# A decode layer streamed through two buffers: a branch to a stub at TensorE's start, one odd row loaded whole, and repeated products in two gaps

## The chip, the core and the metric

The kernel runs on one core of one Trainium2 chip. A core has TensorE (PE in the profile), VectorE (DVE), ScalarE (ACT), GpSimd (POOL) and SyncE (SP), which here issues nearly all the loads, and 16 DMA engines that carry them. The metric is the device time of one execution in microseconds; lower is better. A change of about 0.3% is what a measurement of this kernel can tell from none.

## The reference

One decode step of a transformer layer, in float32, for a batch of 8 tokens with 1024 features:

```python
xn = layernorm(x)                                  # x: 8 x 1024
q = xn @ wq                                        # 32 heads of 128
k, v = last 1024 positions of the caches           # 4 key/value heads, each for 8 heads
p = softmax(q @ k.T * 128 ** -0.5)
h = x + (p @ v) @ wo                               # wo: 4096 x 1024
hn = layernorm(h)
out = h + (gelu(hn @ w_gate) * (hn @ w_up)) @ w_down    # Df = 3584
```

The weights and the caches are 111 MB, each byte of which is used once; the activations are small.

## The kernel before

**Stages.** The weights are rearranged on the host into loads of 128 partitions x 64 KB (8 MB), and two SBUF buffers take them in turn. A pass of TensorE's loop (line 500) uses both: half a (buffer 0, accumulators ob[0]) and half b (buffer 1, ob[1]). The passes are wq, the keys, the values, wo, gate and up for 2048 columns (GU0), gate and up for the other 1536 (GU1, pass 5), and the down projection (DN, pass 6), which has a half a only. W_down has 28 blocks of 128 rows: the first 8 travel in the unused quarter of GU1's loads, 16 are DN's half a, and the last four come behind it.

**A half.** `products` (line 481) goes through 8 steps of four products. The four of a step stand side by side in the array, each with 32 columns of the stationary operand, and write four groups of 32 partitions of an accumulator. Before the steps listed in `cuts` TensorE waits. DN's loads come in three pieces, wd0, wd1 and wd2 (5, 2 and 1 steps; `CUTS`), and TensorE waits ahead of steps 0, 5 and 7. Between the halves `turn` (line 470) transposes the activations. What TensorE waits for is collected by GpSimd, which waits for the semaphores in TensorE's order and raises a single one, `go` (lines 452 to 462).

**Repeated products.** At the places in `AGAIN` TensorE repeats a product with the residual whose result is in fin already (line 479), n times in a small loop: two ahead of DN's step 0 and two ahead of its step 5, and four ahead of step 4 of GU1's half b. They change nothing in the output.

**The start.** The loop runs from -1: pass -1 skips the body (line 501) and goes from the loop's end back to its start.

**The loads.** SyncE issues all loads in a written order; one that needs a buffer waits for TensorE's mark that the buffer is free. Behind wd2 come, into buffer 1, the blocks of W_down's last four rows of blocks (from here on rows): the odd row, two single rows (512 KB each, ws1 and ws2), and the last row in two pieces (256 KB each, we0 and we1). The odd row's first half is one load of 128 partitions (w_odd, 256 KB). Its second half (w_low) is folded to 64 partitions of 4 KB and comes in eight loads of 8 partitions, 32 KB each (line 202), at partitions p0, p0 + 4, ... for the p0 of `OFFSETS`. A load of 128 partitions is spread over all 16 DMA engines, each of these over eight. Fifteen tiny loads (`tag`, line 218) follow, which no computation uses.

**The tail.** The odd row makes three products into ob[0] (line 536): one of 128 partitions in column group 0, and for the folded half two of 64 partitions in groups 2 and 3; ScalarE copies the activations of partitions 64 to 127 to at_low for the last one (line 415). VectorE adds ob[0] to d1 (line 427). Then TensorE sums into fin: row ws1, d1 through add2, row ws2 (line 528), and the last row's pieces (line 547). ScalarE copies fin out in two halves (line 431), which two DMAs store.

Of the kernel before, what the change touches and what calls it, by code (L numbers as in the profile page):

```python
# [30 lines left out]
EARLY = 8  # L31
ENDS = (128, 128)
SINGLE = 3
LOW = P // 2
OFFSETS = (0, 1, 2, 3, 32, 33, 34, 35)
TAGS = 15
AGAIN = (((0, DN, 2), (CUTS[1], DN, 2)), ((STEPS // 2, GU1, 4),))


class Flow:  # L40
# [57 lines left out]
    def run(self, engine, make, *waits, mark=True):  # L98
        ins = self.start(engine, make, waits)
        if not mark:  # L100
            return None
        self.done[engine] += 1
        ins.then_inc(self.own[engine], 1)
        self.tell(engine, self.own[engine], self.done[engine])
        return self.own[engine], self.done[engine]

    def move(self, name, out, src, *waits, engine="sync"):
        s = self.sem(name)
        self.start(engine, lambda e: e.dma_start(out, src), waits).then_inc(s, 16)
        self.tell(engine, s, 16)  # L110
        return s, 16
# [19 lines left out]
    return out  # L131


def decode_block(nc, x, w, dn, side, single, ends, outs):
    fl = Flow(nc)
    run, move = fl.run, fl.move
    scale = DH ** -0.5
# [45 lines left out]
    for k in range(1, DN):  # L183
# [11 lines left out]
    landed[DN, 0] = [  # L195
        move(f"wd{i}", buf[0][:, a * NQ * N:b * NQ * N], dn[i], pe(f"a{GU1}"))
        for i, (a, b) in enumerate(zip(CUTS, CUTS[1:]))]
    w_odd, w_low = buf[1][:, 0:N], buf[1][0:LOW, N:N + D]
    odd_in = [move("wo0", w_odd, single[0], pe(f"b{GU1}"))]
    low_in = fl.sem("w_low")  # L200
    for j, p0 in enumerate(OFFSETS):
        nc.sync.dma_start(w_low[p0:p0 + 29:4], side[j]).then_inc(low_in, 16)
    odd_in.append((low_in, 16 * len(OFFSETS)))
    singles = []
    for i in range(1, SINGLE):
        t = buf[1][:, N + i * D:N + (i + 1) * D]
        singles.append((t, move(f"ws{i}", t, single[i])))
    blocks = []
    c0 = 0
    for i, (n, src) in enumerate(zip(ENDS, ends)):  # L210
        a = N + SINGLE * D + NQ * c0
        t = buf[1][:, a:a + NQ * n]
        blocks.append((n, t, move(f"we{i}", t, src)))
        c0 += n
# [158 lines left out]
    at_low = sb("at_low", LOW, 32)  # L373
    wide = st[0].rearrange("p (i c m) -> p i c m", i=STEPS, c=2)

    def widen(i0, i1, *ready):
# [88 lines left out]
    def wait():  # L465
        nc.tensor.wait_ge(go, 1).then_inc(go, -1)  # L466
# [4 lines left out]
    def turn(src):  # L471
        for i in range(NC):
            ins = nc.tensor.transpose(t8[:, i, :], src[:, i * P:(i + 1) * P], ident)  # L473
        marked(ins)
# [22 lines left out]
            if i % (STEPS // 2) == STEPS // 2 - 1:  # L497
                marked(ins)

    with nc.Fori(-1, PASSES, engines=[mybir.EngineType.PE]) as it:  # L500
        with nc.tensor.If(it >= 0):
            wait()
            turn(xs[1])
            products(0, CUTS)
            with nc.tensor.If(it < DN):
                wait()
                turn(xs[0])
                products(1, (0, STEPS // 2))
                with nc.tensor.If(it == WO):
                    wait()  # L510
                    for ch in range(2):
                        ins = nc.tensor.matmul(
                            fin[0:ROWS, ch * N:(ch + 1) * N], to_rows[:, ch, :], y_sb,
                            start=True, stop=True)
                    marked(ins)
                    wait()
                    for ch in range(2):
                        ins = nc.tensor.matmul(  # L518
                            fin[64 * ch:64 * ch + 32, ch * N:(ch + 1) * N],
                            spread.rearrange("p r b -> p (r b)"), h_sb[:, ch * N:(ch + 1) * N],  # L520
                            start=True, stop=True)
                    marked(ins)

    def add(lhs, rhs, *waits, start=False):

        for d_ps, a, b in halves:
            for j in range(NQ):
                run("tensor", lambda e: e.matmul(  # L528
                    d_ps[32 * j:32 * j + 32, :], lhs(j), rhs(j)[:, a:b], start=start, stop=False),
                    *waits, mark=False)  # L530

    odd = LAST - SINGLE
    for i, (q, lhs, t) in enumerate((
            (0, at[:, odd, :], w_odd), (2, at[0:LOW, odd, :], w_low[:, 0:N]),
            (3, at_low, w_low[:, N:2 * N]))):
        tok = run("tensor", lambda e: e.matmul(  # L536
            ob[0][32 * q:32 * q + 32, N:2 * N], lhs, t, start=False, stop=True,
            skip_group_check=True), *odd_in, at_ok, low_ok, mark=(i == 2))
# [80 lines left out]
```

## Time and profile before

| | |
|---|---|
| timed runs | 267.45, 267.75, 268.28 us; median 267.75 |
| profiled execution | 265.81 us, span 264.5 us |
| granted TensorE clock, mean | 0.826 |
| PE busy | 147.1 us (56%) in 1030 instructions |
| DVE, ACT, POOL busy | 28.5, 28.7, 5.3 us |
| read from HBM | 111.19 MB, 421 GB/s over the span |
| queue q1 (SyncE's loads) | 97.9% of 16 engines |
| queue q8 (instruction) | 2 packets, 0.03 MB |

The profile is of one execution. Busy time is given by engine and by line; the timeline lists instructions in order of time, merged where neighbours are alike, with what an engine was idle for in brackets. PE is the matmul part of TensorE, PEq its instruction queue. The chain that ended last is followed back only to 249.32 us, to the start of the down projection. The granted clock says which share of TensorE's full speed the throttle allowed in a stretch. "Us to landing" is the time from a DMA's issue to its last byte.

### The profile page before, as it was taken

Reading aid. Unit: us, or ns where it says so; the run is one execution under the profiler, and the core shown is the slowest. Engines: PE = TensorE matmul, PEld = TensorE weight load, DVE = VectorE, ACT = ScalarE, POOL = GpSimd, SP = SyncE. Lnnn points to the kernel's source line nnn. Section 1 sums busy time; section 2 is a strip of 40 time slices with the busy share of each in tenths; the row PEclk is TensorE's granted clock in tenths of the full one; section 3 lists DMA queues with packets and bytes.
Section 4 is the critical chain, followed back from the end, with each engine's and each line's share of the span. In section 5 each row is a group of like instructions: output and inputs, shape, how many; then the busy total and the mean of one; then the engine's idle time right before and its main releaser. Section 6 shows DMA issues by size and latency. Waiting matters only on the chain. (4 is left out here: it accounts for less than half of the span.)

```text
span 264.5 us, 2418 instructions
## 1 busy us (share of the span) xinstructions
PE 147.1 (56%) x1030; PEld 50.4 (19%) x1030; DVE 28.5 (11%) x47; ACT 28.7 (11%) x50; POOL 5.3 (2%) x11
## 2 busy tenths in 40 slices
PE   0023924814915926617617808728909609957696
PEld 0021311211211221111112302103302202312222
DVE  0310020010010010400400100250000200102011
ACT  1030000020030030010010000033200100200200
POOL 8000000000000000000000000000000000000000
PEclk9999995985985865965975976985885968997999
DMA  8998999899799979998999899799979999999894
GB/s 320 471 456 347 466 476 426 377 466 476 337 466 466 476 327 466 476 456 347 466 476 426 377 466 476 337 466 466 476 322 466 406 456 416 421 429 477 378 402 144
DMA packets 3843, 111.37 MB, mean 421 GB/s; under 512 B 696, under 2 KB 952, under 8 KB 1664
## 3 DMA queue, kind: packets, MB, share of 16 engines
q1 hardware_dynamic: 3680, 111.23, 97.9%
q10 hardware_dynamic: 160, 0.10, 0.1%
q8 instruction: 2, 0.03, 0.1%
q14 instruction: 1, 0.01, 0.0%
HBM read 111.19 MB, written 0.13 MB: 421 GB/s over the span
## 5 line engine op out<-in xcount | busy, mean ns | idle before, releaser
L493 PE MATMUL o<-w,st 128*32 128x512 f32 x832 | 118.0, 725 | 76.5 <-PEq L466 70.1
L493 PEld LDWEIGHTS o<-w,st 128*32 128x32 f32 x832 | 33.0, 130 | 153.0 <-issue 152.9
L473 PE MATMUL tt<-ident,zeros 128*128 128x128 f32 x104 | 16.5, 311 | 36.0 <-PEq L466 36.0
L473 PEld LDWEIGHTS tt<-ident,zeros 128*128 128x128 f32 x104 | 13.3, 159 | 46.4 <-issue 46.4
L479 PE MATMUL fin<-zeros,spread 128*32 128x512 f32 x16 | 7.4, 594 | 0.0
L330 DVE SCALAR_TENSOR_TENSOR av<-o,rtot,own 128x512 f32<-128x512 f32 x4 | 3.0, 750 | 31.3 <-PE o L493 31.3
L313 DVE TENSOR_REDUCE nmax<-o 128x1 f32<-128x1024 f32 x2 | 2.4, 1224 | 35.3 <-PE o L493 35.3
L340 ACT COPY st<-tt 128x512 f32<-128x512 f32 x4 | 2.1, 588 | 35.4 <-PE tt L473 35.4
L315 ACT ACTIVATE zeros<-o,nmax 128x1024 f32<-128x1024 f32 x2 | 2.2, 1114 | 33.6 <-DVE nmax L313 33.6
L355 DVE TENSOR_TENSOR y_sb<-o,y_sb 128x512 f32<-128x512 f32 x3 | 2.1, 692 | 34.2 <-PE o L493 34.2
L295 DVE SCALAR_TENSOR_TENSOR zeros<-o,tq 128x512 f32<-128x512 f32 x2 | 1.4, 692 | 36.1 <-PE o L493 36.1
L399 DVE TENSOR_TENSOR u<-o,u 128x512 f32<-128x512 f32 x2 | 1.4, 692 | 31.8 <-PE o L493 31.8
L390 DVE TENSOR_TENSOR g<-o,g 128x512 f32<-128x512 f32 x2 | 1.4, 691 | 29.4 <-PE o L493 29.4
L294 ACT ACTIVATE tq<-o 128x512 f32<-128x512 f32 x2 | 1.2, 597 | 23.9 <-PE o L493 23.9
L333 DVE TENSOR_REDUCE zeros<-av 128x128 f32<-128x1024 f32 x2 | 3.7, 1872 | 0.1
L362 ACT COPY zeros<-fin 32x512 f32<-32x512 f32 x1 | 0.6, 574 | 26.4 <-PE fin L518 26.4
L226 POOL MEMSET zeros<- 128x3712 f32 x1 | 3.2, 3191 | 0.0
L405 ACT COPY at<-tt 128x512 f32<-128x512 f32 (+1 forms) x2 | 1.1, 532 | 19.3 <-PE tt L473 19.3
L389 ACT COPY g<-o 128x512 f32<-128x512 f32 x2 | 1.2, 586 | 16.2 <-PE o L493 16.2
L262 ACT ACT_TABLE_LOAD x2 | 2.6, 1283 | 2.9 <-POOL ident L223 2.9
L278 ACT COPY st<-tt 128x1024 f32<-128x1024 f32 x2 | 2.0, 1012 | 7.7 <-PE tt L473 7.7
L398 ACT COPY u<-o 128x512 f32<-128x512 f32 x2 | 1.2, 586 | 14.4 <-PE o L493 14.4
(60 smaller groups left out, 43.6 us busy)
## 6 DMA issues: line engine op xcount, KB each, us to landing
w<-ends SPq DMA_DIRECT2D x4, 4096.0 KB, 23.4
w<-ends SPq DMA_DIRECT2D x1, 5120.0 KB, 22.8
w<-ends SPq DMA_DIRECT2D x1, 2048.0 KB, 27.3
w<-ends SPq DMA_DIRECT2D x1, 1024.0 KB, 29.3
w<-ends SPq DMA_DIRECT2D x2, 512.0 KB, 10.6
w<-ends SPq DMA_DIRECT2D x3, 256.0 KB, 11.3
w<-ends SPq DMA_DIRECT2D x8, 32.0 KB
w<-w SPq DMA_DIRECT2D x10, 29.3
```

The lines of the kernel that those rows point to most:

```text
L226: clear = run("gpsimd", lambda e: e.memset(zeros, 0.0))
L262: tok = run("scalar", lambda e: e.activation(sd, ve, AF.Sqrt), tok)
L278: a = run("scalar", lambda e: e.copy(st[0].rearrange("p (c r b) -> p c r b", c=NC, b=B), xt.unsqueeze(2).to_broadcast([P, NC, P // B, B])) ...
L313: tok = run("vector", lambda e: e.tensor_reduce(out=nmax, in_=ob[s], axis=AX.X, op=ALU.max, negate=True), pe(f"{h}1"))
L315: tok = run("scalar", lambda e: e.activation(xs[s], ob[s], AF.Exp, bias=nmax, accum_out=tot), tok)
L330: tok = run("vector", lambda e: e.scalar_tensor_tensor(av[:, i], o3, rtot, own.unsqueeze(2).to_broadcast([P, HB, DH]), op0=ALU.mult, op1=A ...
L333: tok = run("vector", lambda e: e.tensor_reduce(out=out, in_=av.rearrange("p i b d -> p d (i b)"), axis=AX.X, op=ALU.add), tok)
L340: tok = run("scalar", lambda e: e.copy(heads[:, g], turned.unsqueeze(2).to_broadcast([P, REP, P // 2 // B, B])), pe(f"t{h}2"))
L355: tok = run("vector", lambda e: e.tensor_add(y_sb, part, y_sb), ready, tok)
L473: ins = nc.tensor.transpose(t8[:, i, :], src[:, i * P:(i + 1) * P], ident)
L479: nc.tensor.matmul(fin[0:32, 0:N], spread.rearrange("p r b -> p (r b)"), h_sb[:, 0:N], start=True, stop=True)
L493: ins = nc.tensor.matmul(ob[s][32 * r:32 * r + 32, c:c + N], st[s][:, i * P + 32 * r:i * P + 32 * r + 32], buf[s][:, (i * NQ + r) * N:(i * ...
```

## The change

Four things are done.

1. The loop runs from 0, without a test for pass -1. Ahead of it TensorE branches to a block "far", which holds only a branch to "near", where the loop begins. "far" is written inside the test for pass `WO`, behind its products; a branch to "behind" goes around it.
2. The odd row isn't folded. It is loaded as one load of 128 partitions x 4 KB, as the single rows are, so buffer 1 holds three single rows, and w_odd, w_low and the eight small loads go.
3. The odd row makes two products of 128 partitions, in column groups 0 and 2; at_low and its copy go.
4. `AGAIN`: DN has three repeated products ahead of step 0 and none ahead of step 5; GU1's half b has six.

The core of the diff:

```diff
-LOW = P // 2
-OFFSETS = (0, 1, 2, 3, 32, 33, 34, 35)
-AGAIN = (((0, DN, 2), (CUTS[1], DN, 2)), ((STEPS // 2, GU1, 4),))
+AGAIN = (((0, DN, 3),), ((STEPS // 2, GU1, 6),))
...
-    w_odd, w_low = buf[1][:, 0:N], buf[1][0:LOW, N:N + D]
-    odd_in = [move("wo0", w_odd, single[0], pe(f"b{GU1}"))]
-    low_in = fl.sem("w_low")
-    for j, p0 in enumerate(OFFSETS):
-        nc.sync.dma_start(w_low[p0:p0 + 29:4], side[j]).then_inc(low_in, 16)
-    odd_in.append((low_in, 16 * len(OFFSETS)))
     singles = []
-    for i in range(1, SINGLE):
-        t = buf[1][:, N + i * D:N + (i + 1) * D]
-        singles.append((t, move(f"ws{i}", t, single[i])))
+    for i in range(SINGLE):
+        t = buf[1][:, i * D:(i + 1) * D]
+        singles.append((t, move(f"ws{i}", t, single[i], pe(f"b{GU1}"))))
...
-            low_ok = run("scalar", lambda e: e.copy(at_low, at[LOW:P, LAST - SINGLE, :]), at_ok)
...
-    with nc.Fori(-1, PASSES, engines=[mybir.EngineType.PE]) as it:
-        with nc.tensor.If(it >= 0):
+    only = [mybir.EngineType.PE]
+    entry = nc.cur_bb
+    nc.tensor.br("far")
+    nc.switch_bb("near")
+    with nc.Fori(0, PASSES, engines=only) as it:
...
+                nc.tensor.br("behind")
+                with nc.body("far", parent=entry, valid_engines=only):
+                    nc.tensor.br("near")
+                nc.switch_bb("behind")
...
-    for i, (q, lhs, t) in enumerate((
-            (0, at[:, odd, :], w_odd), (2, at[0:LOW, odd, :], w_low[:, 0:N]),
-            (3, at_low, w_low[:, N:2 * N]))):
+    for ch in range(2):
         tok = run("tensor", lambda e: e.matmul(
-            ob[0][32 * q:32 * q + 32, N:2 * N], lhs, t, start=False, stop=True,
-            skip_group_check=True), *odd_in, at_ok, low_ok, mark=(i == 2))
+            ob[0][64 * ch:64 * ch + 32, N:2 * N], at[:, odd, :], t[:, ch * N:(ch + 1) * N],
+            start=False, stop=True, skip_group_check=True), here, at_ok, mark=(ch == 1))
```

The built programs are listed by engine, in the order in which the instructions stand. TensorE at the loop's start, before; COMPARE_AND_BRANCH of L501 is the test for pass -1, the rows of L487 to L478 are the repeated products ahead of steps 0 and 5:

```order
L500 UNCONDITIONAL_BRANCH
L501 COMPARE_AND_BRANCH
L473 MATMUL tt<-ident,zeros 128x128 x8
L487 COMPARE_AND_BRANCH
L478 UNCONDITIONAL_BRANCH
L479 MATMUL fin<-zeros,spread 32x512
L478 REGISTER_ALU
L478 COMPARE_AND_BRANCH
L487 UNCONDITIONAL_BRANCH
L493 MATMUL o<-w,st 32x512 x20
L487 COMPARE_AND_BRANCH
L478 UNCONDITIONAL_BRANCH
```

The same place after (L492 is the branch ahead of the loop, L494 the loop):

```order
L492 UNCONDITIONAL_BRANCH
L494 UNCONDITIONAL_BRANCH
L463 MATMUL tt<-ident,zeros 128x128 x8
L477 COMPARE_AND_BRANCH
L468 UNCONDITIONAL_BRANCH
L469 MATMUL fin<-zeros,spread 32x512
L468 REGISTER_ALU
L468 COMPARE_AND_BRANCH
L477 UNCONDITIONAL_BRANCH
L483 MATMUL o<-w,st 32x512 x32
```

The test for pass -1 is gone, and the products of steps 0 to 7 stand in one piece. TensorE at the loop's end and the start of the tail, before (L512 and L518 are pass `WO`'s products, L500 the loop's end, L536 the odd row, L528 the sums):

```order
L509 COMPARE_AND_BRANCH
L512 MATMUL fin<-y_sb,zeros 64x512 x2
L518 MATMUL fin<-zeros,spread 32x512 x2
L509 UNCONDITIONAL_BRANCH
L500 REGISTER_ALU
L500 COMPARE_AND_BRANCH
L536 MATMUL o<-w,at 32x512 x2
L536 MATMUL o<-w,at_low 32x512
L528 MATMUL fin<-w,at 32x128 x8
L528 MATMUL fin<-d,add 32x128 x8
```

And after:

```order
L502 COMPARE_AND_BRANCH
L505 MATMUL fin<-y_sb,zeros 64x512 x2
L511 MATMUL fin<-zeros,spread 32x512 x2
L516 UNCONDITIONAL_BRANCH
L494 REGISTER_ALU
L494 COMPARE_AND_BRANCH
L532 MATMUL o<-w,at 32x512 x2
L525 MATMUL fin<-w,at 32x128 x8
L525 MATMUL fin<-d,add 32x128 x8
```

The branch to "behind" (L516) stands where the test's own branch stood; a row of the stub's branch (line 518) is not among TensorE's. The odd row has two products instead of three. SyncE's loads from wd0 on, before:

```order
L109 DMA w0<-ends 128x10240
L109 DMA w0<-ends 128x4096
L109 DMA w0<-ends 128x2048
L109 DMA w1<-ends 128x512
L202 DMA w1<-ends 8x1024 x8
L109 DMA w1<-ends 128x1024 x2
L109 DMA w1<-ends 128x512 x2
```

And after:

```order
L107 DMA w0<-ends 128x10240
L107 DMA w0<-ends 128x4096
L107 DMA w0<-ends 128x2048
L107 DMA w1<-ends 128x1024 x3
L107 DMA w1<-ends 128x512 x2
```

Nine loads, of the odd row in two forms, have become one. The bytes are the same.

More of the change, by code (lines that the diff above doesn't have):

```diff
@@ L131, in pe_order, with decode_block @@
     return out
-def decode_block(nc, x, w, dn, side, single, ends, outs):
+def decode_block(nc, x, w, dn, single, ends, outs):
     fl = Flow(nc)
@@ L210, in decode_block @@
     for i, (n, src) in enumerate(zip(ENDS, ends)):
[L211 removed]
+        a = SINGLE * D + NQ * c0
         t = buf[1][:, a:a + NQ * n]
@@ L498, in products @@
                 marked(ins)
-    with nc.Fori(-1, PASSES, engines=[mybir.EngineType.PE]) as it:
-        with nc.tensor.If(it >= 0):
+    only = [mybir.EngineType.PE]
[3 more added lines that the diff above has]
+    with nc.Fori(0, PASSES, engines=only) as it:
+        wait()
+        turn(xs[1])
+        products(0, CUTS)
+        with nc.tensor.If(it < DN):
             wait()
-            turn(xs[1])
-            products(0, CUTS)
-            with nc.tensor.If(it < DN):
+            turn(xs[0])
+            products(1, (0, STEPS // 2))
+            with nc.tensor.If(it == WO):
                 wait()
[L507 to L522, printed above, removed]
+                for ch in range(2):
+                    ins = nc.tensor.matmul(
+                        fin[0:ROWS, ch * N:(ch + 1) * N], to_rows[:, ch, :], y_sb,
+                        start=True, stop=True)
+                marked(ins)
+                wait()
+                for ch in range(2):
+                    ins = nc.tensor.matmul(
+                        fin[64 * ch:64 * ch + 32, ch * N:(ch + 1) * N],
+                        spread.rearrange("p r b -> p (r b)"), h_sb[:, ch * N:(ch + 1) * N],
+                        start=True, stop=True)
+                marked(ins)
+                nc.tensor.br("behind")
+                with nc.body("far", parent=entry, valid_engines=only):
+                    nc.tensor.br("near")
+                nc.switch_bb("behind")
     def add(lhs, rhs, *waits, start=False):
@@ L530, in add @@
                     *waits, mark=False)
+    (t, here), *singles = singles
     odd = LAST - SINGLE
[L533 to L535 removed]
+    for ch in range(2):
         tok = run("tensor", lambda e: e.matmul(
[L537 to L538 removed]
+            ob[0][64 * ch:64 * ch + 32, N:2 * N], at[:, odd, :], t[:, ch * N:(ch + 1) * N],
+            start=False, stop=True, skip_group_check=True), here, at_ok, mark=(ch == 1))
     assert tok == odd_done
@@ L585 @@
     parts += [main[:, a * NQ:b * NQ] for a, b in zip(CUTS, CUTS[1:])]
-    odd = down[:, LAST - SINGLE]
-    low = odd[:, 1].reshape(2, LOW, N).transpose(1, 0, 2)
-    parts += [np.stack([low[p0:p0 + 29:4] for p0 in OFFSETS]), odd[:, 0]]
-    parts += [down[:, i] for i in range(LAST - SINGLE + 1, LAST)]
+    parts += [down[:, i] for i in range(LAST - SINGLE, LAST)]
     parts += [row[:, :, a:b] for a, b in zip(cuts, cuts[1:])]
@@ L609 @@
     w = [aps["w"][i] for i in range(2 * GU1)] + small[0:4]
-    dn, side, single, ends = small[4:7], small[7], small[8:8 + SINGLE], small[8 + SINGLE:]
-    side = side.rearrange("p n -> (p n)").rearrange("(j r n) -> j r n", j=len(OFFSETS), r=8)
-    decode_block(nc, aps["x"], w, dn, side, single, ends, outs)
+    dn, single, ends = small[4:7], small[7:7 + SINGLE], small[7 + SINGLE:]
+    decode_block(nc, aps["x"], w, dn, single, ends, outs)
     r = run_bass_kernel_spmd(nc, [arrays], core_ids=[0])
```

1 line of the change is left out of this document (removed).

## Prediction

> **What bounds the kernel now.** I read the page's slices and queues first, then TensorE's timeline from 226 us, the DMA issues, and the busy time in stretches of 3.41 us.
>
> The page: what the DMA engines do, and what each load takes from issue to landing.
>
> ```profile
> DMA  8998999899799979998999899799979999999894
> q1 hardware_dynamic: 3680, 111.23, 97.9%
> q8 instruction: 2, 0.03, 0.1%
> w<-ends SPq DMA_DIRECT2D x1, 5120.0 KB, 22.8
> w<-ends SPq DMA_DIRECT2D x1, 2048.0 KB, 27.3
> w<-ends SPq DMA_DIRECT2D x1, 1024.0 KB, 29.3
> w<-ends SPq DMA_DIRECT2D x2, 512.0 KB, 10.6
> w<-ends SPq DMA_DIRECT2D x3, 256.0 KB, 11.3
> ```
>
> The loads fill 16 engines almost all the time: up to the last 15 us the kernel is a stream of 111 MB that TensorE waits for. Only the tail, after the last large load, can be shortened by an engine. SyncE's timeline gives the issue times to add to these waits.
>
> ```profile
> 226.43 16.53 SPq L109 DMA_DIRECT2D w<-ends  x4
> 248.50 1.86 SPq L109 DMA_DIRECT2D w<-ends  x4
> ```
>
> The first three of the four at 226.43 are the W_down loads wd0, wd1 and wd2, about 0.44 us apart, so they land at 226.43 + 22.8 = 249.2, 226.87 + 27.3 = 254.2 and 227.31 + 29.3 = 256.6. The four at 248.50 stand 0.46 apart; the last lands at 249.90 + 11.3 = 261.2.
>
> TensorE's timeline from the up projection to the end (start, us, what):
>
> ```profile
> 230.95 3.60 PE L479 MATMUL fin<-zeros,spread 128*32 128x512 f32 x8
> 237.25 5.34 PE L493 MATMUL o<-w,st 128*32 128x512 f32 x32 [2.69 <-PEq L466]
> 244.32 1.06 PE L473 MATMUL tt<-ident,zeros 128*128 128x128 f32 x8 [1.74 <-PEq L466]
> 245.32 1.90 PE L479 MATMUL fin<-zeros,spread 128*32 128x512 f32 x4
> 249.36 4.50 PE L493 MATMUL o<-w,st 128*32 128x512 f32 x40 [2.14 <-PEq L466]
> 253.65 1.45 PE L479 MATMUL fin<-zeros,spread 128*32 128x512 f32 x3
> 254.94 0.59 PE L479 MATMUL fin<-zeros,spread 128*32 128x512 f32 x1
> 254.97 3.14 PE L493 MATMUL o<-w,st 128*32 128x512 f32 x21
> 257.94 1.56 PE L536 MATMUL o<-w,at 128*32 128x512 f32 x3
> 259.35 0.59 PE L536 MATMUL o<-w,at_low 64*32 64x512 f32 x1
> 260.81 0.65 PE L528 MATMUL fin<-d,add 128*32 128x128 f32 x16 [0.29 <-DVE mark L434]
> 261.70 0.62 PE L547 MATMUL fin<-w,at 128*32 128x128 f32 x16
> ```
>
> Four products stand side by side in the array and take two passes; I call one pass of four a slot. Ten slots (x40) run from 249.36 to 253.65, so a slot is 0.43 us at full clock. A repeated product is two slots that use a quarter of the array. From 249.36 the chain is: five steps (10 slots), two repeated products (4 slots), steps 5 and 6 (4), step 7 (2), the odd row (L536), an add on VectorE, and sums. Its end is set by TensorE: the last load is there at 261.2, TensorE reaches the last sums at 261.70. VectorE and ScalarE close it:
>
> ```profile
> 260.06 0.69 DVE L427 TENSOR_TENSOR d<-o,d 128x512 f32<-128x512 f32 x1 [6.24 <-PE o L536]
> 262.17 0.48 ACT L431 COPY o_fin<-fin 128x128 f32<-128x128 f32 x2 [14.74 <-PE fin L547]
> 262.69 0.35 ACTq L109 DMA_DIRECT2D out<-o_fin  x1
> ```
>
> The profiled execution took 265.81 us (span 264.5). The three timed runs took 267.45 to 268.28, median 267.75: 1.6 to 2.5 us more. I sum against 265.81 first and come back to that gap, because the change acts on it.
>
> **The branch and the stub.** The rows of TensorE's order hold the branch of line 492 and nothing of line 518: the stub is an empty detour that the program no longer contains, and TensorE goes straight into pass 0. [...]
>
> ```profile
> q8 instruction: 1, 0.02, 5.2%
> ```
>
> One 16 KB fetch takes 5.2% of 16 engines for 1.1 us, 0.92 us of one engine, in the stream. [...] What it is late by at the end can be read from the DMA share (columns: stretch, its length, busy us of PE, PEld, DVE, ACT and POOL with counts, granted PE clock, DMA share, GB/s):
>
> ```profile
> 257.20:258.20 1.00, 1.00 (x10) 0.22 (x2) 0.00 (x0) 0.00 (x0) 0.00 (x0) 1.00 1.04 410
> 259.40:260.20 0.80, 0.80 (x16) 0.33 (x16) 0.14 (x1) 0.00 (x0) 0.00 (x0) 1.00 0.59 225
> 260.60:261.20 0.60, 0.39 (x16) 0.40 (x20) 0.15 (x2) 0.00 (x0) 0.00 (x0) 1.00 0.07 8
> ```
>
> From 259.4 on 0.59 of 16, nine engines, still read. Eight are those of the small loads, which gave each 8 x 4 KB = 32 KB that the others don't have; the ninth has only been late all along, by about as much as 32 KB take. 111.23 MB in 97.9% of 264.5 us are 430 GB/s, 27 per engine, so 32 KB take 1.2 us. I take 1.2 us for the lag, before and after, since it is the whole effect of such a fetch in this stream; its lower bound is the packet alone, 0.92, its upper bound is rival 4.
>
> **No small loads.** On SyncE eight issues and w_odd's become one, which brings the later issues from 248.50 to about 243.5; their data come behind wd2, 256.6, either way, so the data stream hides it. What changes is the late engine's share: 512/16 = 32 KB for the odd row where it had 256/16 = 16 KB. That is +0.6 us on it from there on. The odd row lands at 256.6 + 1.2 = 257.8, the last block at 261.2 + 0.6 = 261.8.
>
> The odd row itself gets shorter. Today the 128-row product and the two 64-row products don't overlap: 257.94 to 259.35 + 0.59 = 259.94, 2.00 us. Two 128-row products in different columns share slots, as those of L493 do: 2 slots, 0.43 + 0.59 = 1.02 us. (If they did not overlap it would be 4 slots, 1.9 us: that is the upper bound, and no loss against today.) Also the ScalarE copy into at_low goes, 0.22 us that wait for nothing.
>
> Sum at this execution's clock: start 257.8 + 0.1 = 257.9, end 258.9, add on VectorE (0.12 later, 0.69 long) to 259.75, its sums from 259.8 instead of 260.81. Now the loads come last: the last block at 261.8, its eight instructions 0.1 later, their last start about 261.95 to 262.0 where today it is 262.05. So 1.0 us won on TensorE is given back to the late engine and the end moves by -0.1 us: 265.7.
>
> **The repeated products.** Three instead of two ahead of the down projection end 0.86 us later, at 248.1, still before 249.2: free here. Six instead of four in the up projection fill 230.95 to 236.1, the load is used from 237.25: free too. Two in the middle of the last pass go: 4 slots, 1.7 us, off the chain. At this execution's clock that shows as little (steps 5 to 7 then wait for wd1 at 254.2 and wd2 at 256.6, and end at 257.8 instead of 258.1). It shows when the clock is low. Granted clock and TensorE's busy time in stretches on which the clock changes (same columns):
>
> ```profile
> 70.58:73.99 3.41, 1.50 (x16) 0.27 (x8) 1.23 (x1) 0.58 (x1) 0.00 (x0) 1.00 0.84 365
> 73.99:77.40 3.41, 1.07 (x8) 0.86 (x8) 0.16 (x1) 1.63 (x3) 0.00 (x0) 1.00 0.75 327
> 77.40:80.81 3.41, 0.00 (x0) 0.00 (x0) 0.00 (x0) 0.00 (x0) 0.00 (x0) 0.50 1.38 596
> 179.80:183.22 3.42, 2.15 (x14) 0.57 (x16) 0.00 (x0) 2.06 (x2) 0.00 (x0) 0.50 0.75 326
> 183.22:186.63 3.41, 3.41 (x24) 0.91 (x20) 0.00 (x0) 0.00 (x0) 0.00 (x0) 0.50 1.15 500
> 217.35:220.76 3.41, 2.85 (x16) 0.90 (x20) 0.00 (x0) 0.00 (x0) 0.00 (x0) 0.50 1.03 442
> 220.76:224.18 3.42, 3.42 (x36) 1.07 (x32) 0.00 (x0) 0.59 (x1) 0.00 (x0) 1.00 0.96 412
> 234.41:237.83 3.42, 0.72 (x9) 0.34 (x12) 0.00 (x0) 0.00 (x0) 0.00 (x0) 1.00 0.88 381
> 237.83:241.24 3.41, 3.41 (x24) 1.09 (x16) 0.00 (x0) 0.00 (x0) 0.00 (x0) 0.50 1.20 517
> 241.24:244.66 3.42, 1.68 (x15) 0.53 (x8) 1.38 (x2) 0.00 (x0) 0.00 (x0) 1.00 1.03 443
> ```
>
> The changes fall on a grid of 3.41 us. Full clock falls to half behind a stretch with 0.72 or 1.07 us of work and holds behind 1.50; half clock holds behind 2.15 us of work and rises behind 2.85. I put the limits between: 1.3 us to fall, 2.5 us to rise. Nothing ties this grid to the kernel's start in the rows, so in another execution it may lie elsewhere. Put it 1.1 us later. Then 235.51 to 238.92 holds 1.7 us of work, the clock stays full, and the four steps from 237.25 take 3.6 instead of 5.34 us. Everything up to the repeated products is 1.75 us earlier; they end at 245.5. The stretch 245.76 to 249.17 is empty, and 249.17 to 252.58 runs at half clock: 3.22 us / 0.86 = 3.8 slots, the other 6.2 at 0.43, five steps done at 255.3 instead of 253.65. Ten more slots bring the odd row to 259.55 instead of 257.94. From there on all is one chain: the end is 1.6 us later. That is about the gap between 265.81 and the timed median. Working the same steps through for 18 places of the grid, the kernel before ends 1.4 to 2.5 us later in 12 of them.
>
> After the change the same place gives: six repeated products until 236.1, full clock, three until 246.3, half clock from 249.17 too, five steps done at 255.3. But then only six slots follow: step 7 leaves the array at 257.9, when the odd row's load lets it start anyway. The cost is nothing; over the 18 places it is at most 0.1 us.
>
> [...]
>
> **The rivals.** (1) Forecast: the timed runs before are mostly at such places of the grid. Then 267.75 - 1.6 - 0.1 = 266.05, say 266.1. For it: the gap has the right size in all three runs (1.64, 1.94, 2.47). Against it: one profiled execution shows one place only. Chance 0.52.
>
> (2) The gap is something else that profiled and timed executions differ by, and stays. Then only the -0.1 us counts: 267.65, no change that can be told (0.3%, 0.8 us, is about what a measurement of this kernel can tell). Chance 0.35.
>
> (3) The stub is run after all, and the fetch comes before the stream instead of inside it: in the trace it lies at 5 us, a few us behind the first load's start. The late engine then isn't late, every load lands up to 1.2 us earlier: 264.9 on top of (1), 266.45 on top of (2). Against it: the order has no such branch. Chance 0.03.
>
> [...] Chance 0.10. [...]
>
> **How the numbers follow.** The time is that of (1), 266.1. Its own range is 265.2 (a place that costs 2.5 today) to 266.4 (1.4, with a lag of the upper half). The range must reach (2), 267.65 with 0.25 around it: 265.2 to 267.9. Faster by over 0.3% takes (1) and (3), 0.55; the same is (2), 0.35; slower is (4), 0.10.
>
> **What would show it.** Right: a 16 KB fetch away from 5 us, near 45; odd products of about 1.0 us; the sums on d before 260.2; the last sums waiting for their load; a span of 264.2 to 264.6 wherever the clock's changes lie, with five steps at half clock costing nothing. Wrong: a fetch at 2 us or none, several fetches, a last landing after 262.2, or timed runs that again lie 2 us above the profiled one.

## The result, and the profile after

The changed kernel takes 265.71 us (median of five runs, 265.51 to 265.87) where the kernel before takes 267.45 in the five runs beside it (267.28 to 268.28): a ratio of 0.9928, 95% interval 0.9912 to 0.9944. The profiled execution took 265.51 us with a span of 264.0; before it was 265.81 and 264.5. So the two profiles lie 0.3 us apart, the timed runs 1.7. Where the other 1.4 us are, no comparison of the two profiles can show.

The page of the changed kernel: the DMA slices, the queues, the chain that ended last, and the loads (us from issue to landing).

```profile
DMA  8997998999799979999997999799989999999994
...
q8 instruction: 2, 0.03, 0.1%
...
DMA 7%; PE 2%; SPq 1%; issue 0%; ACT 0%
DMA w<-ends 7%; PE o L483 1%; SPq L107 1%; PE fin L543 0%; ACT o_fin L421 0%
...
w<-ends SPq DMA_DIRECT2D x3, 512.0 KB, 17.8
...
w<-ends SPq DMA_DIRECT2D x2, 256.0 KB, 18.9
```

SyncE's timeline (start, us, what):

```profile
227.01 15.99 SPq L107 DMA_DIRECT2D w<-ends  x8
```

The chain that ended last now consists mostly of loads (DMA 7% of the span, TensorE 2%); before, it was TensorE's work from the down projection on. The small loads take longer from issue to landing because they are issued earlier: all eight loads by 243.0, where the last four used to start at 248.50.

TensorE's timeline from the up projection to the end:

```profile
231.36 5.31 PE L469 MATMUL fin<-zeros,spread 128*32 128x512 f32 x12
237.08 3.64 PE L483 MATMUL o<-w,st 128*32 128x512 f32 x32 [0.40 <-PEq L456]
242.46 1.06 PE L463 MATMUL tt<-ident,zeros 128*128 128x128 f32 x8 [1.74 <-PEq L456]
243.45 2.76 PE L469 MATMUL fin<-zeros,spread 128*32 128x512 f32 x6
249.19 8.77 PE L483 MATMUL o<-w,st 128*32 128x512 f32 x64 [2.98 <-PEq L456]
257.82 1.05 PE L532 MATMUL o<-w,at 128*32 128x512 f32 x4
259.00 0.64 PE L525 MATMUL fin<-w,at 128*32 128x128 f32 x16
259.72 0.64 PE L525 MATMUL fin<-d,add 128*32 128x128 f32 x16
260.29 0.65 PE L525 MATMUL fin<-w,at 128*32 128x128 f32 x16
260.92 0.43 PE L543 MATMUL fin<-w,at 128*32 128x128 f32 x8
261.61 0.42 PE L543 MATMUL fin<-w,at 128*32 128x128 f32 x8 [0.27 <-DMA w<-ends]
```

The odd row (L532) takes 1.05 us instead of 2.00. The sums on d (L525) start at 259.72 instead of 260.81, and the last piece (L543) waits for its load. ScalarE's timeline closes it: the two halves of the output are copied apart, where before both came in one stretch. The last store is issued at 262.40 instead of 262.69 and lands after 1.6 us instead of 1.8; together that is the 0.5 us between the spans.

```profile
261.41 0.27 ACT L421 COPY o_fin<-fin 128x128 f32<-128x128 f32 x1 [16.08 <-PE fin L543]
262.11 0.27 ACT L421 COPY o_fin<-fin 128x128 f32<-128x128 f32 x1 [0.43 <-PE fin L543]
262.40 0.35 ACTq L107 DMA_DIRECT2D out<-o_fin  x1
```

The clock, in stretches of its grid, and a stretch at the end of the loads (columns as in the prediction):

```profile
242.57:245.98 3.41, 3.41 (x14) 1.29 (x13) 0.00 (x0) 1.72 (x3) 0.00 (x0) 1.00 1.17 504
245.98:249.39 3.41, 0.43 (x5) 0.19 (x8) 0.00 (x0) 0.00 (x0) 0.00 (x0) 1.00 0.73 310
249.39:252.81 3.42, 3.42 (x20) 1.09 (x16) 0.00 (x0) 0.00 (x0) 0.00 (x0) 0.50 0.97 410
260.50:260.85 0.35, 0.35 (x16) 0.16 (x8) 0.00 (x0) 0.00 (x0) 0.00 (x0) 1.00 0.06 23
```

Behind the stretch with 0.43 us of work the clock falls, and the first steps of the down projection run at half clock from 249.39 to 252.81. This is the place that the prediction works out as dear for the kernel before. Here the 16 slots of L483 end at 249.19 + 8.77 = 257.96, the odd row follows at 257.82 (the two rows of the timeline overlap by 0.14 us), and the last sums still wait 0.27 us for their load. So the half clock does not reach the end. In the last row a share of 0.06 of the 16 DMA engines still reads: one engine is late.

The queues between 48 and 50 us:

```profile
q8 instruction: 1, 0.02, 3.3%
```

3.3% of 16 engines for 2 us is 1.06 us of one engine: the 16 KB fetch, which stood between 5.0 and 6.1 us in the kernel before, where it took 0.92 us.

### The profile page after: what moved, and what is told of

Same layout as the page of the kernel before. It is cut to its first block, busy times and chain, and to the rows that moved or that the text cites. A ratio compares the mean times of both kernels' runs of the same rounds, so it can differ in the third digit from the quotient of the medians.

```text
span 264.0 us, 2392 instructions
## 1 busy us (share of the span) xinstructions
PE 151.5 (57%) x1030; PEld 51.9 (20%) x1030; DVE 28.6 (11%) x47; ACT 28.6 (11%) x49; POOL 5.4 (2%) x11
## 5 line engine op out<-in xcount | busy, mean ns | idle before, releaser
L483 PE MATMUL o<-w,st 128*32 128x512 f32 x832 | 119.1, 736 | 71.7 <-PEq L456 67.1
L483 PEld LDWEIGHTS o<-w,st 128*32 128x32 f32 x832 | 33.0, 131 | 150.5 <-issue 150.5
L463 PE MATMUL tt<-ident,zeros 128*128 128x128 f32 x104 | 18.3, 334 | 35.9 <-PEq L456 35.9
L463 PEld LDWEIGHTS tt<-ident,zeros 128*128 128x128 f32 x104 | 14.7, 172 | 46.3 <-issue 46.3
L469 PE MATMUL fin<-zeros,spread 128*32 128x512 f32 x18 | 8.1, 593 | 0.0
L469 PEld LDWEIGHTS fin<-zeros,spread 128*32 128x32 f32 x18 | 1.9, 110 | 5.3 <-issue 5.3
```

The source lines that it names most:

```text
L469: nc.tensor.matmul(fin[0:32, 0:N], spread.rearrange("p r b -> p (r b)"), h_sb[:, 0:N], start=True, stop=True)
L483: ins = nc.tensor.matmul(ob[s][32 * r:32 * r + 32, c:c + N], st[s][:, i * P + 32 * r:i * P + 32 * r + 32], buf[s][:, (i * NQ + r) * N:(i * ...
```

## The experiments

**Theory A**, the prediction's: the kernel before has two kinds of executions, according to where the 3.41-us grid of the clock lies. In most of them the first five steps of the down projection run at half clock, and since the two repeated products and an odd row of 2.0 us stand behind them, the delay reaches the end. The change takes both away. The rivals are that the odd row's shape alone counts, that the fetch and the loads count, or that profiled and timed executions differ in something else. Each expectation names the rivals that it tells apart. There were 12 runs; the kernel before was timed beside most of them. The ratios compare means, so they move with how many runs of the kernel before fall into its lower group; the medians and single times say more here.

**The kernel before itself.** All its timed runs in this study, 95, make two groups with nothing between them: 28 from 265.65 to 266.24 (median 265.95) and 67 from 267.03 to 269.10 (median 267.62). Both profiled executions of it (265.81, and 265.68 when it was profiled once more, below) belong to the lower group. The gap between profiled and timed time is a gap between two groups of executions, and timed runs fall into both.

The record has the span and the mean granted clock of 90 of these runs. Span x 2 x (1 - clock) / 3.41 is then the number of stretches at half clock (264.5 us at 0.826 give 27.0), and it comes out whole, within 0.1, in every run. Of 13 runs with 27 stretches 12 are in the lower group, of 14 with 28 none, of 47 with 29 fourteen, of 16 with 30 or 31 two. So the group goes with the course of the clock in the timed runs themselves, which a cause that has nothing to do with the clock would not bring about. Where in the run the stretches lie these figures don't say. The extra time lies inside the span: the time outside it is 1.3 to 1.5 us in both groups, but for two runs with 2.0.

**No repeated products inside the last pass** (kernel before).

```diff
-AGAIN = (((0, DN, 2), (CUTS[1], DN, 2)), ((STEPS // 2, GU1, 4),))
+AGAIN = (((0, DN, 2),), ((STEPS // 2, GU1, 4),))
```

> The kernel before without the two repeated products in the middle of the last pass; all else as before, four repeated products in the up projection included. Theory A (the timed runs of before mostly run the five steps of the last pass partly at half clock, and the four slots behind them then stand on TensorE's chain to the end): the slots go from the chain, 267.45 - 1.65 = 265.8 us, between 265.6 and 266.1. Theory B (the gain comes from the odd row, which is loaded and multiplied in another shape; repeated products lie in waits): no change, 267.3 to 267.6. Theory C (the loads bound the end, and the gain comes from where the instruction fetch lies): no change either.

Measured: median 266.47 in 12 runs, ratio 0.9971 (0.9949 to 0.9994). Seven runs lie from 265.77 to 266.06 and five from 266.89 to 267.35. In the profiled execution, one of the lower seven, the half clock lay over the first steps (the 16 slots took 8.77 us from 249.24, as in the changed kernel's profile), they ended at 258.0, and the last sums started at 261.56: without the two products that place costs nothing. So the upper group comes down from 267.62 to about 267.1 and becomes smaller, but it doesn't vanish as expected: these two products are a part of the matter, not all of it.

**One repeated product instead of four in the up projection** (kernel before).

```diff
-AGAIN = (((0, DN, 2), (CUTS[1], DN, 2)), ((STEPS // 2, GU1, 4),))
+AGAIN = (((0, DN, 2), (CUTS[1], DN, 2)), ((STEPS // 2, GU1, 1),))
```

> The kernel before with one repeated product instead of four in the up projection's gap; the two in the middle of the last pass stay. Theory A: TensorE then idles 5 us ahead of the second half of the up projection, so the clock falls there wherever the grid lies, the half runs slowly and ends late, the gap ahead of the last pass is short, and the last pass starts at full clock: most executions end 1.6 us earlier, median about 265.9 us, a few still at 267.4. Fewer filling products make it faster. Theory B and C: no change, 267.3 to 267.6. The usual reading that filling products keep the clock up for what follows: slower or the same.

Measured: median 266.79, 265.79 to 267.89, ratio 0.9989 (0.9962 to 1.0017). Six of 12 runs lie over 267. The expectation was that the clock, made to fall ahead of the four up steps, would seldom fall again before the down projection. In the profiled execution it did as expected; in half of the runs something cost 1 to 2 us. No trace of such a run was taken, so this stays open. By the ratio the runs can't be told from no change.

**The odd row whole, nothing else** (kernel before, with the load and the two products of the change).

```diff
...
-            (0, at[:, odd, :], w_odd), (2, at[0:LOW, odd, :], w_low[:, 0:N]),
-            (3, at_low, w_low[:, N:2 * N]))):
+    for ch in range(2):
...
+            ob[0][64 * ch:64 * ch + 32, N:2 * N], at[:, odd, :], t[:, ch * N:(ch + 1) * N],
...
```

> The kernel before with only the odd row loaded whole and multiplied in two products; loop from -1 and repeated products as before. Theory A: the ten slots behind the five steps stay on the chain, only the odd row's own two slots go: -0.9 to -1.0 us, 266.5 us, no more. Theory B: the whole gain, 265.7 us. Theory C: no change, or 0.6 us slower since the late DMA engine has 16 KB more.

Measured: median 266.60, 265.49 to 267.46, ratio 0.9974 (0.9951 to 0.9998), as expected. The odd row alone is worth about half of the change. Its profiled execution (266.45 us) had the half clock over the first steps (its ten slots took 6.20 us, against 4.50 in the profile of the kernel before), with the two products behind them:

```profile
249.21 6.20 PE L483 MATMUL o<-w,st 128*32 128x512 f32 x40 [3.83 <-PEq L456]
...
262.28 0.62 PE L536 MATMUL fin<-w,at 128*32 128x128 f32 x16
```

From the first step to the last sums that is 13.1 us, where the kernel before takes 12.3 in its profile, although its odd row is 0.95 us longer.

**The stub kept in the program** (changed kernel, with an instruction in the stub that does nothing, so that the build keeps the detour).

```diff
                 with nc.body("far", parent=entry, valid_engines=only):
+                    nc.tensor.nop(nofuse=True)
                     nc.tensor.br("near")
```

> [...] If the 16 KB fetch gets ahead of the first load's packets, no DMA engine is late by 1.1 us, and as the loads bound the end of the changed kernel, it ends 1.1 us earlier: 264.6 us. If the fetch falls behind the first packets, near 5 us as before, the late engine is late as now: 265.7 us, and with theory C 266 to 267. The profile shows which: the fetch at 2 us or at 5.

Measured: median 265.61, 265.05 to 265.92, ratio 0.9944 (0.9924 to 0.9964). The fetch now stands between 1.5 and 3.5 us:

```profile
q8 instruction: 1, 0.02, 4.4%
```

That is 1.41 us of one engine, at the start of the stream. TensorE's timeline and a stretch of the end:

```profile
257.36 1.05 PE L533 MATMUL o<-w,at 128*32 128x512 f32 x4 [0.17 <-DMA w<-ends]
261.16 0.43 PE L544 MATMUL fin<-w,at 128*32 128x128 f32 x8 [0.24 <-DMA w<-ends]
```

```profile
260.40:260.80 0.40, 0.39 (x12) 0.16 (x8) 0.06 (x1) 0.00 (x0) 0.00 (x0) 1.00 0.04 11
```

One engine is late here too (a share of 0.04 still reads), and the last piece is there 0.45 us earlier than in the changed kernel (261.16 against 261.61). But the whole end lies earlier by that much, from the first step of the down projection on (248.73 against 249.19), and profiles of kernels with the fetch in one place differ as much (249.19 for the changed kernel, 249.75 with two products put back, below). Rival 3 of the prediction gave this case 1.2 us. The medians differ by 0.1 to 0.2 us, which these runs can't tell from nothing, so that a gain from the early fetch is not shown.

**The clock made to fall ahead of the down projection** (kernel before, only the two products inside the last pass kept).

```diff
-AGAIN = (((0, DN, 2), (CUTS[1], DN, 2)), ((STEPS // 2, GU1, 4),))
+AGAIN = (((CUTS[1], DN, 2),), ())
```

> The kernel before, with the repeated products of both gaps taken out and the two inside the last pass kept, so that the clock falls ahead of the down projection wherever its grid lies. Theory A (half clock in the first five steps, and a TensorE chain with no room behind them): no run at 265.9 any more; all runs from 267.0 to 268.7, median 268; in the trace the first five steps take 5.9 us or more, the odd row starts at 259 or later, the span is 266 or more. Theory B (the gap between the profiled and the timed runs has nothing to do with the clock): the same as the kernel before, 267.5, with about a quarter of the runs at 266.

Measured: median 268.64, 267.61 to 269.58, ratio 1.0046 (1.0018 to 1.0075). The lower group is gone. The stretches of the clock and TensorE's timeline of the profiled execution (268.98 us, span 267.6):

```profile
245.19:248.60 3.41, 0.81 (x8) 0.57 (x6) 0.00 (x0) 1.93 (x4) 0.00 (x0) 1.00 0.97 416
248.60:252.01 3.41, 2.49 (x12) 0.68 (x16) 0.00 (x0) 0.00 (x0) 0.00 (x0) 0.50 0.95 406
252.01:255.43 3.42, 3.42 (x20) 0.90 (x16) 0.00 (x0) 0.00 (x0) 0.00 (x0) 0.50 1.00 405
```

```profile
249.52 7.41 PE L493 MATMUL o<-w,st 128*32 128x512 f32 x40 [3.52 <-PEq L466]
256.74 1.45 PE L479 MATMUL fin<-zeros,spread 128*32 128x512 f32 x3
...
258.06 3.14 PE L493 MATMUL o<-w,st 128*32 128x512 f32 x21
261.03 1.56 PE L536 MATMUL o<-w,at 128*32 128x512 f32 x3
...
264.79 0.62 PE L547 MATMUL fin<-w,at 128*32 128x128 f32 x16
```

This is the chain that the prediction worked out for the dear place, seen in a trace, with two stretches at half clock where the prediction had one. Ten slots take 7.41 us instead of 4.50, the odd row starts at 261.03 instead of 257.94, and the last sums at 264.79 instead of 261.70. It also shows that 2.49 us of work in a stretch don't bring the clock back, so that it can stay low for two stretches in a row.

**The changed kernel without repeated products.**

```diff
-AGAIN = (((0, DN, 3),), ((STEPS // 2, GU1, 6),))
+AGAIN = ((), ())
```

> The changed kernel without any repeated product. Theory A: half clock in the first five steps costs nothing, because no repeated product and only two odd slots stand behind them: 265.7, within 0.2 of the changed kernel; the trace shows half clock over the first steps and the same end. Rival: the nine repeated products are what makes the changed kernel even; then 266.5 or more, and a spread of over 1 us.

Measured: median 266.42, 265.43 to 267.48, ratio 0.9963 (0.9939 to 0.9987): the expectation by A failed, and the rival's numbers came. The profiled execution, the fastest of the twelve, had the half clock over the first steps (16 slots in 8.73 us from 249.15) and the end of the changed kernel (the last piece's sums at 261.53, against 261.61). Of the seven runs over 266.4 us, four (266.43 to 266.96) have spans of 263.8 to 264.1 us, as short as the quick ones'. They lose their time outside the span: 2.6 to 3.0 us of it, where the runs of all kernels otherwise have 1.3 to 1.6 and three of them 2.0. What happens there no profile shows. The other three have spans of 265.0 to 266.0; the second profile of this kernel, below, is of that kind.

**Two repeated products put back into the last pass** (changed kernel).

```diff
-AGAIN = (((0, DN, 3),), ((STEPS // 2, GU1, 6),))
+AGAIN = (((0, DN, 3), (CUTS[1], DN, 2)), ((STEPS // 2, GU1, 6),))
```

> The changed kernel with two repeated products put back in the middle of the last pass. Theory A: four slots more on the chain, of which the shorter odd row takes up two: 265.7 at about two fifths of the clock's places, up to 266.4 at the rest, median 266.2. Theory B (only the odd row's shape counts): 265.7, no spread.

Measured: median 266.45, 265.56 to 267.99, ratio 0.9963 (0.9938 to 0.9987): nearer to A than to B, but six of the 12 runs lie above the 266.4 at which A had them end. The profiled execution took 267.06 us with a span of 265.5. Its clock fell for one stretch, as in the changed kernel's profile:

```profile
249.88:253.29 3.41, 3.41 (x20) 1.11 (x19) 0.00 (x0) 0.00 (x0) 0.00 (x0) 0.50 0.94 396
```

TensorE's timeline:

```profile
249.75 6.20 PE L483 MATMUL o<-w,st 128*32 128x512 f32 x40 [2.99 <-PEq L456]
255.73 1.45 PE L469 MATMUL fin<-zeros,spread 128*32 128x512 f32 x3
...
257.05 2.71 PE L483 MATMUL o<-w,st 128*32 128x512 f32 x20
...
261.92 0.64 PE L525 MATMUL fin<-d,add 128*32 128x128 f32 x16 [0.43 <-DVE mark L424]
...
262.81 0.62 PE L543 MATMUL fin<-w,at 128*32 128x128 f32 x16
```

The same fall of the clock that costs the changed kernel nothing costs time here. The last store is issued at 263.80, 1.4 us later than in the changed kernel's profile. Of that, 0.56 us are there already when the steps start (249.75 against 249.19) and have nothing to do with the products; the other 0.8 come behind them, where the two products of L469 stand. The medians of the two kernels differ by 0.6. The last sums no longer wait for a load, and from the first step to the last sums it is 13.1 us, as with the odd row alone.

**Only the table of repeated products changed** (kernel before, with the table of the change).

```diff
-AGAIN = (((0, DN, 2), (CUTS[1], DN, 2)), ((STEPS // 2, GU1, 4),))
+AGAIN = (((0, DN, 3),), ((STEPS // 2, GU1, 6),))
```

> The kernel before with only the table of repeated products changed: six and three in the gaps, none in the last pass; the odd row keeps its three products. Theory A by slots alone: 265.8, all runs within 0.2. By the run that took out the two inside the last pass and kept four and two in the gaps (266.5, in two groups at 265.9 and 267.1): two groups again, median 266.5; then something besides the five steps runs at half clock in the upper group. Theory B (the odd row's shape alone): 267.4.

Measured: median 266.09, ratio 0.9962 (0.9937 to 0.9987); ten of 12 runs from 265.80 to 266.38, and one each at 267.06 and 267.96. This is near to A by slots, which had 265.8 and all runs within 0.2; ten runs spread over 0.6 and two lie above them. The table alone brings 1.4 of the 1.7 us. Six and three in the gaps do better than four and two (ten of 12 low runs instead of seven, a difference that 12 runs hardly prove). One stretch of its clock bears on the limit of the fall:

```profile
247.29:250.70 3.41, 1.31 (x13) 0.52 (x17) 0.00 (x0) 0.00 (x0) 0.00 (x0) 1.00 0.92 394
250.70:254.11 3.41, 3.41 (x21) 1.09 (x17) 0.00 (x0) 0.00 (x0) 0.00 (x0) 0.50 0.99 416
```

Behind 1.31 us of work the clock fell; the prediction's rows had it hold behind 1.50. The limit lies between them, or isn't sharp in these busy times: in the profile with one repeated product the clock held behind about 1.3 us. That is an estimate from its timeline: the 5.21 us of the up steps from 237.24 put the end of their half clock at 240.4, three stretches of 3.41 us later is 250.6, 1.3 us behind the start of the ten slots at 249.34, and these took 4.50 us, all at full clock.

**The changed kernel again.** No edit.

> The changed kernel as it is, on this chip and beside the runs below. Theory A (the clock's place no longer counts): all runs within 0.5, median 265.7. Theory B (the first five runs were lucky, and the spread of the kernels without fill is that of the chip): runs up to 267, median 266 or more.

Measured: median 265.86 in 12 runs, 265.61 to 266.38, ratio 0.9956 (0.9930 to 0.9983; ten of the 23 runs of the kernel before beside it fell into the lower group). With the first five that makes 17 runs from 265.51 to 266.38, median 265.83: one group. The 12 runs spread over 0.8 us, where A expected 0.5.

**Only the loop and the branch changed** (kernel before).

```diff
-    with nc.Fori(-1, PASSES, engines=[mybir.EngineType.PE]) as it:
-        with nc.tensor.If(it >= 0):
+    only = [mybir.EngineType.PE]
+    entry = nc.cur_bb
+    nc.tensor.br("far")
+    nc.switch_bb("near")
+    with nc.Fori(0, PASSES, engines=only) as it:
...
```

> The kernel before with only the loop and the branch changed. If the place of the fetch doesn't count: 267.5 in two groups, as before. If the fetch inside the stream makes one engine later than the fetch at its start: 0.3 to 0.6 slower. If it gains: 267.0 or less. The trace shows the fetch near 48 us.

Measured: median 267.36 beside 267.47, ratio 1.0001 (0.9969 to 1.0033), four runs at 266 and eight from 267.05 on. The fetch stands at 48 to 50 us in this trace as well (3.3% of 16 engines, 1.06 us of one), and none between 3 and 7 us. The place of the fetch does nothing to the time that these runs can tell.

**The kernel before, profiled once more.**

> The kernel before, profiled once more. Theory A: where this execution takes 267 or more, the first steps of the down projection run at half clock, steps 5 to 7 end behind the odd row's load and the odd row starts at 259 or later; where it takes 266, the half clock lies elsewhere, as in the first profile. Rival (the profiled execution differs from timed ones in something else): 266 again with the half clock in the first five steps, or 267.5 without it.

Measured: 265.68 us, the lower group again. Its clock, and TensorE's timeline:

```profile
234.79:238.21 3.42, 1.07 (x12) 0.50 (x16) 0.00 (x0) 0.00 (x0) 0.00 (x0) 1.00 1.19 513
238.21:241.62 3.41, 3.41 (x20) 1.07 (x16) 0.00 (x0) 0.00 (x0) 0.00 (x0) 0.50 1.03 444
```

```profile
249.26 4.50 PE L493 MATMUL o<-w,st 128*32 128x512 f32 x40 [2.15 <-PEq L466]
```

The half clock lies over the up projection, and the five steps run at full clock, as theory A has it for the lower group. An execution of the upper group of this very kernel was not caught in a trace; what it looks like is inferred from the kernels beside it. The sizes fit: half clock over one stretch and the two products make 13.1 us from the first step to the last sums in two traces (the odd row alone, and the two products put back); with the 0.95 us that the old odd row is longer an estimate for the kernel before is 14.0, 1.7 more than the 12.3 of its profile, and the groups lie 1.67 apart.

**The changed kernel without repeated products, profiled once more.**

> The changed kernel without repeated products, profiled once more, to see what its upper runs do. If two stretches in a row stay at half clock over the steps of the down projection (the first of them not full of work): the odd row starts at 258.5 or later, the span is 264.5 or more and the time 266.3 to 267.3. If the loads are late instead: the odd row lands after 258.2 and the clock is as in the first profile. At 265.7 the look tells nothing new.

Measured: 267.33 us, span 265.8, so one of its longer executions was caught, and it is neither of the two cases expected. TensorE's timeline is that of the changed kernel:

```profile
249.28 8.77 PE L483 MATMUL o<-w,st 128*32 128x512 f32 x64 [2.72 <-PEq L456]
...
261.65 0.43 PE L543 MATMUL fin<-w,at 128*32 128x128 f32 x8 [0.23 <-DMA w<-ends]
```

The time is lost behind it. The output's two stores, by the view of the tile o_fin (us from issue to landing), in the changed kernel's profile:

```profile
DMA to landing us min/median/max: 1.6/1.6/1.7
```

and in this execution, with what its instruction queue did between 263 and 265 us:

```profile
DMA to landing us min/median/max: 1.6/2.5/3.4
```

```profile
q8 instruction: 1, 0.02, 4.7%
```

The second store takes 3.4 us instead of 1.6. A 16 KB fetch (4.7% of 16 engines for 2 us, 1.5 us of one engine) lies between 263 and 265 us, just where that store, issued at 262.4, would land after 1.6 us. In the changed kernel's own profile the last fetch lies between 261 and 263 us, mostly ahead of the store's data:

```profile
q8 instruction: 1, 0.02, 3.4%
```

In the quick execution of this kernel (265.43 us) the page counts one packet on this queue, where the pages of before, after and this execution have two, and between 260 and 266 us its queues list none:

```profile
q8 instruction: 1, 0.02, 0.0%
```

So this longer run, as far as one trace shows, is not the clock's doing: a 16 KB fetch of 1.5 us at the program's end lies over the last store, which takes 1.8 us longer. The trace can stand for at most the three timed runs with a longer span; the four that lose their time outside the span stay open. What sets the place of this fetch no run shows.

## Why the prediction was right

*The stub.* The detour is out of the program, the fetch is away from 5 us and comes inside the stream, between 48 and 50 us where the forecast had 45; it costs nothing that the runs can tell (ratio 1.0001 with the loop and the branch alone). Where it lies follows the change at TensorE's start in four profiles: 5 us in the kernel before, 48 to 50 with the loop and the branch changed and in the changed kernel, 1.5 to 3.5 with the detour kept in the program. What sets these places no run shows; the 45 us were the author's estimate. Rival 4, several fetches in the stream (chance 0.10), did not come: the changed kernel's page counts two packets on the instruction queue, one between 48 and 50 us and one between 261 and 263, with six jumps back of the loop. So no run shows the second fetch in the stream that the forecast took for the upper bound of the lag.

*The late engine and the loads.* The odd row starts at 257.82 (said: 257.9), the last block's sums at 261.61 (said: last block landed at 261.8, its sums 0.1 later). The lag was over-sized: the last sums start 0.3 us earlier than forecast. That the forecast of 266.1 lies 0.4 us above the 265.71 measured has another reason for the most part: it started from 267.75, the median of three runs, and the five runs beside the result have 267.45.

*The odd row.* 1.05 us against 1.02 said, sums on d at 259.72 against 259.8. The loads took back only a part of the 1.0 us: between the two profiles the time moved by 0.3 and the span by 0.5, where the sum had 0.1. The last store is issued 0.3 us earlier, since the lag was over-sized, and lands 0.2 us faster.

*The repeated products and the clock.* This step carried the forecast, and the runs bear it out, the part in the kernel before by inference (no execution of its upper group is in a trace). The working had the kernel before late at 12 of 18 places of the grid, by 1.4 to 2.5 us and 1.6 in the example; 67 of 95 runs are in an upper group whose median is 1.67 us above the lower one. Rival 2 (the gap stays) fell with 17 runs of the changed kernel in one group. The kernel with no repeated products in the two gaps, in whose profile the clock falls (ten slots in 7.41 us instead of 4.50), lost the lower group altogether (267.61 to 269.58). That the shares agree so well is in part luck: the working had a limit for the rise that a trace puts higher.

*What was mis-sized.* The forecast gave the whole step to the two products inside the last pass. Taken out alone they brought 1.0 us and left an upper group; the odd row alone brought 0.9. That both are halves of one thing, the number of slots behind the five steps, fits these sizes (1.9 together, 1.7 for the whole change); it is argued, not shown. The limits were also off: 1.3 us for the fall is at the edge (behind 1.31 it fell in the profile with only the table changed), and 2.5 for the rise was too low (behind 2.58 it stayed low in the second profile without repeated products, and behind 2.85 it rose in the kernel before). The stretch of 2.58, at half clock, was followed by more of it: the 32 products from 237.16 took 6.59 us, against 3.64 at full clock in the changed kernel:

```profile
236.32:239.74 3.42, 2.58 (x15) 0.73 (x19) 0.00 (x0) 0.00 (x0) 0.00 (x0) 0.50 1.30 563
```

With the one for the rise higher there are more places at which two stretches in a row stay at half clock. As an estimate, put a change at 247.8, with the five steps from 249.36: the first stretch then holds 1.8 us of work and the clock comes back at 254.6. Until then 5.24 / 0.86 = 6.1 slots are done; the other 3.9 end at 256.3, and six more bring the odd row to 258.9, 1.0 us late even without the two products. That would fit the runs at 267 that are left in the kernels with only one half of the change; it was worked out, not seen in them. "At most 0.1 us" for the changed kernel was short: its 17 runs spread over 0.9, and what spreads them was not looked into.

## What to carry to other kernels

When the timed runs lie above the profiled one, collect many times of the same kernel first: two groups with a gap, here 28 and 67 runs with medians 1.67 us apart, say that something with states of its own decides, and one profile shows only one of them. Give the end of a kernel room of its own, fewer instructions behind the last large load, rather than trying to keep the clock up: then it matters less where the clock falls (the 17 runs of the changed kernel lie within 0.9 us, the 95 of the kernel before within 3.5). Filler is free only in a gap that ends before the next data arrive, as the three ahead of the down projection do here (246.2 us, steps from 249.19); behind that point it stands on the chain, as the two products put back into the last pass did (0.6 us between the medians).

## What was not expected of the hardware

- The clock falls behind stretches that are far from idle: behind 1.31 us of work in 3.41 it fell in one trace (only the table changed), behind 1.50 it held in another (the kernel before), and behind 2.58 it did not come back (the second profile without repeated products). Ahead of TensorE's first products with a load (24.20 us in the kernel before) the column shows 1.00 with hardly any work: none from 20.00 to 24.20 us.
- A 16 KB fetch at the end of the program lay over a store of 64 KB in one execution (the second profile without repeated products): 3.4 us to landing instead of 1.6, and a time of 267.33 us instead of 265.43.
- In three profiles with a fetch in the stream one engine was late at the end: the fetch took one engine 1.41 us at 2 us, 0.92 at 5 us and 1.06 at 48 us, and 0.04, 0.07 and 0.06 of 16 engines still read.
